# A fused delta-rule attention and two MoE layers: the first four chunks' norms split, their first loads and T's spread rewritten

## The chip, the cores and the metric

The kernel runs on one core of one Trainium2 chip. The metric is the device time of one execution in microseconds (us). The kernel before was run three times: 1037.36, 1038.86 and 1046.35 us, median 1038.86.

## The reference, cut to what matters

Inputs are q, k, v of shape (B=4, H=8, S=768, D=48), beta (B, H, S) and two pairs of weight matrices of 384 x 2048 and 2048 x 384.

```python
k_n = k / (np.linalg.norm(k, axis=-1, keepdims=True) + 1e-06)
state = np.zeros((B, H, D, D))
for t in range(S):
    y[:, :, t] = einsum('bhd,bhde->bhe', q[:, :, t], state)
    v_old = einsum('bhde,bhd->bhe', state, k_n[:, :, t])
    state += beta_t * einsum('bhd,bhe->bhde', k_n[:, :, t], v[:, :, t] - v_old)
x = y as rows of (B*S, H*D)
h = x @ w1_in;  x = softplus(h) @ w1_out
h = x @ w2_in;  x = (h * cos(h)) @ w2_out
```

So every key vector is divided by its norm, a recurrence over 768 steps makes y, and two dense layers with different activations follow.

## The kernel before

The 768 steps are cut into NS = 24 chunks of C = 32 steps, and the chunks into NG = 6 groups of four. Partitions hold 4 batches x 32 steps. All values that reach TensorE (PE) are pairs of f16 (a high part and a rest, called hi and lo), so a product takes three passes.

For a group g the work is: `norms(g)` loads the four K tiles kt0 to kt3 and makes 1/(norm + 1e-6) for all four chunks in n0 (a square on ScalarE, a sum over 48 on VectorE, then a square root by Ln and Exp with one Newton step, on 128 x 32 elements). `prep_k(n)` scales kt by n0, splits it into kp (hi, lo) and transposes it in 32 x 32 blocks. `gram(n)` multiplies K by K and Q by K on PE against block-diagonal copies (bdK, bdQ, bdA, bd2). `take_A`, `take_P` take the result out; `solve(g)` inverts the triangular systems of the four chunks together on VectorE, row by row (tmpd and tlan), and writes T: t16, then tg by a transpose, then DRAM. `step(n)` is the recurrence of chunk n: it uses T from bdT, and bdG, bd2, bdK and bdQ, loaded from DRAM. The results y16 of two chunks make one block of x for the first dense layer, `moe_block(0, j)`; the second layer, `moe_block(1, j)`, comes last. `weights(ph)` loads the 16 weight pieces of 768 KB each (`conv`, f = 0 to 15) and turns each into hi and lo with three VectorE instructions on 128 x 768 words (L456, L458, L460), a hi copy (L471 on ScalarE or L475 on VectorE) and a lo (L481). Piece 0 goes through the buffer raw, piece 1 through w8, piece 2 through w10.

For the first group there is a path of its own: the transposed K of chunks 0 to 3 goes into the tail of two weight buffers (w12, w14), and sixteen small loads of 48 KB (SBUF to SBUF, one for each of two tiles, two halves and four batches) spread it over bdK, bdQ, bdA and bd2; T of chunk 0 is spread over bdT by four copies on 32 partitions instead of through DRAM.

The order of the instructions on each engine is not the order of the code: the class `Plan` collects all operations with costs and dependences, runs a list scheduler with its own estimates (among them one for each DMA), and issues everything in the order that it found. An operation that two engines can do goes to the one that the planner picks. So a changed dependence or cost number moves instructions in the whole program. On the chip each engine, and SP and ScalarE as issuers of DMAs, runs its list strictly in order, and waits where an operand is not ready.

Of the kernel before, what the change touches and what calls it, by code (L numbers as in the profile page):

```python
# [10 lines left out]
F32 = mybir.dt.float32  # L11
# [3 lines left out]
AF = mybir.ActivationFunctionType  # L15
ALU = mybir.AluOpType
AX = mybir.AxisListType
# [3 lines left out]
P = 128  # L21
# [4 lines left out]
DM = H * D  # L26
# [30 lines left out]
class Plan:  # L57
# [59 lines left out]
    @staticmethod  # L117
    def after(o):

        return 0.65 + 0.9 + o["dma"] + o["slack"] if o["var"][0][0] == "SP" else 0.0  # L120

    def tails(self, succ):
        ops = self.ops
# [9 lines left out]
    def greedy(self, tail, succ, pred, back=None):  # L133
# [34 lines left out]
        while len(log) < n:  # L168
# [55 lines left out]
            if e == "SP" and back is None:  # L224
# [44 lines left out]
def dve(n, fast=False):  # L269
    return 0.068 + n / (1920.0 if fast else 960.0)  # L270
# [15 lines left out]
def delta_moe_moe_kernel(ctx, tc, q, k, v, beta, mask, w1, w2, out):  # L286
# [89 lines left out]
    def put(var, w, r, fn, **kw):  # L376
        return pl.add(var, w, r, fn, **kw)

    def dma(dst, src, w, r, eng_us, issue=0.475, **kw):
        put([("SP", issue)], w, r, lambda e: nc.sync.dma_start(out=dst, in_=src), dma=eng_us, **kw)  # L380
# [60 lines left out]
    cvn = [0]  # L441

    def conv(ph, f, t, key):
        put([("SP", 0.475)], key, [("wp2",)] if ph else [],
            lambda e: nc.sync.dma_start(out=t(), in_=(w1, w2)[ph][f]), dma=2.18)
        c = cvn[0] % NCV
        cvn[0] += 1
        cv = cvb[c]
        cf = cv.bitcast(F32)
        n = 2 * DM  # L450
        ck = [("cv", c, 0), ("cv", c, 1)]

# [24 lines left out]
        def lo(e):  # L477
            if ph:
                eng[e].tensor_tensor(out=wv(1), in0=cf, in1=wv(0), op=ALU.subtract)
            else:  # L480
                nc.vector.scalar_tensor_tensor(wv(1), in0=cf, scalar=sc, in1=wv(0), op0=ALU.mult, op1=ALU.subtract)  # L481

        put([("ACT", act(n)), ("DVE", dve(n, True))], wk, ck, hi, port=True)
        put([("POOL", pool(n)), ("DVE", dve(n))][0 if ph else 1:], wk, ck, lo, port=True)


    def norms(g):
        ss, n0, rn = nrm
        NK = [("n0",)]
        for n in range(4 * g, 4 * g + 4):  # L490
            s = n % 4
            kt = ktb[s]
            kk = [("kt", s)]
            dma(kt, k[n].rearrange("p (h d) -> p h d", h=H), kk, [("pre",)], 0.55, **A)
            if g:
                sqv, qk = sq, ("sq",)
            else:
                sqv, qk = (gb + eb)[s].rearrange("p a t -> p (a t)")[:, 0:DM].rearrange(
                    "p (h d) -> p h d", h=H), (("g", 0), ("g", 1), ("e", 0), ("e", 1))[s]
            actf(sqv, kt, AF.Square, [qk], kk + [("pre",)], DM, **A)  # L500
            put([("DVE", dve(DM))], [("ss", s)], [qk, ("pre",)],
                lambda e, s=s, sqv=sqv: nc.vector.reduce_sum(out=ss[:, s], in_=sqv, axis=AX.X), **A)
        SS = [("ss", i) for i in range(4)]
        m = 4 * H
        actf(n0, ss, AF.Ln, NK, SS + [("tiny",)], m, bias=tiny, **A)
        actf(n0, n0, AF.Exp, NK, [], m, scale=0.5, **A)
        put([("DVE", 0.269)], [("rn",)], NK, lambda e: nc.vector.reciprocal(out=rn, in_=n0), **A)
        tt(rn, rn, ss, ALU.mult, [("rn",)], SS, m, only=("DVE",), **A)
        tt(n0, n0, rn, ALU.add, NK, [("rn",)], m, only=("DVE",), **A)
        put([("DVE", 0.085)], NK, [], lambda e: nc.vector.tensor_scalar(  # L510
            n0, n0, 0.5 / K_SC, 1e-6 / K_SC, op0=ALU.mult, op1=ALU.add), **A)
        put([("DVE", 0.269)], NK, [], lambda e: nc.vector.reciprocal(out=n0, in_=n0), **A)

    def prep_k(n):
        s = n % 4
        kt, kp, kq = ktb[s], kpb[s], kqb[s]
        kk = [("kt", s)]
        tt(kt, kt, nrm[1][:, s].unsqueeze(2).to_broadcast([P, H, D]), ALU.mult, kk, [("n0",), ("pre",)], DM, pool_c=0.79, **A)
        ka = kab[n % 2]
        kr = kk + [("pre",)]  # L520

# [48 lines left out]
    def k_keys(n):  # L570
        return [("kq", n % 4, 0), ("kq", n % 4, 3)] if n >= 4 else [("kg", n, 0), ("kg", n, 1)]
# [64 lines left out]
    def solve(g):  # L636
# [17 lines left out]
        for j in range(N2 - 1):  # L654
# [14 lines left out]
        put([("DVE", 1.135)], [("tg",)], [("t16", 0), ("t16", 1)] + PR,  # L669
            lambda e: nc.vector.transpose(out=gw, in_=tw_), **A)  # L670
        if g == 0:
            for b in range(B):
                rows = slice(32 * b, 32 * b + 32)
                copy(bdT[rows, :, b], tg[rows, 0].rearrange("p h i x -> p h (i x)"), 1.0, [("bdT", b)],
                     [("tg",), ("bdT", "z")] + PR, 512, **A)
# [271 lines left out]
    for n in range(4):  # L947
        prep_k(n)
        if n % 2:
            dst, keys = (bdKQ[:, :, 0:12], bdA22)[n // 2], [first[n - 1][1], first[n][1]]  # L950
            src = kg0[n // 2][:, :, 16 * C:].rearrange("p n (x t) -> p n x t", t=X2)
            for m in range(2):
                for b in range(B):
                    rows = slice(32 * b, 32 * b + 32)
                    dma(dst[rows, m, :, b], src[rows, m], [(keys[m], b)],
                        k_keys(n - 1 + m) + [(keys[m], "z")], 0.5, issue=0.65, **A)
    for n in range(4):
        ps, pk = gram(n, first[n][0], first[n][1], (0,))
        take_A(n, ps[:, :, 0], pk)
# [92 lines left out]
```

## Time and profile before

| what | value |
|---|---|
| runs | 1037.36, 1038.86, 1046.35 us, median 1038.86 |
| profiled execution, span from first to last instruction | 1038.4 us; nothing else of that execution's time is given |
| PE busy, share of the span | 940.7 us, 91% |
| VectorE (DVE), ScalarE (ACT), GpSimd (POOL) | 668.8, 667.2, 366.2 us |
| PE's first matmul | 19.24 us |
| PE's first matmul of `step(0)` | 50.70 us |
| mean granted TensorE clock | 0.965 of full |

The profile is of one execution. Its span lies between the two lower runs, so the span can be read as the time of the kernel. Rows of a timeline give the start, the duration, the engine, the line of the kernel, the operation, output and inputs, and in square brackets how long the engine had stood idle and what released it; a number behind x is how many instructions were merged into a row.

### The profile page before, as it was taken

The numbers are of one execution on the slowest core, as the hardware profiler recorded it, in microseconds if no ns is written. First come the engines' busy times: TensorE is split into PE (matmuls) and PEld (weight loads), VectorE is DVE, ScalarE is ACT, GpSimd is POOL, SyncE is SP. The second block draws the span as 40 slices with busy tenths as digits, with TensorE's granted clock in tenths as the row PEclk, the third lists the DMA queues.
The fourth block names the chain that finished last, engine by engine and source line by source line (L and its number), as shares of the span: only waits on it lengthen the run. The fifth ranks groups of instructions, "written<-read, shape, count | busy, mean of one in ns | idle before, by whom it ended". The sixth has DMA issues, their size and how long they took to land.

```text
span 1038.4 us, 27814 instructions
## 1 busy us (share of the span) xinstructions
PE 940.7 (91%) x11552; PEld 687.5 (66%) x11552; DVE 668.8 (64%) x1186; ACT 667.2 (64%) x1261; POOL 366.2 (35%) x330
## 2 busy tenths in 40 slices
PE   1135889997999899999999999999999999999998
PEld 1125779886899798899999997744444444444443
DVE  8999977666547754863576665686555555555454
ACT  5344769776767776866777787865555555554554
POOL 3013326433523442432332545553332223233232
PEclk9965899998999999999999999999999999999999
DMA  6998696876766775674558862111001010000000
GB/s 194 288 262 203 128 240 121 200 177 170 175 84 149 178 155 111 135 157 76 117 115 210 237 153 84 44 35 61 31 1 61 1 61 0 31 31 1 31 1 31
DMA packets 307741, 117.94 MB, mean 114 GB/s; under 512 B 272160, under 2 KB 287648, under 8 KB 307616
## 3 DMA queue, kind: packets, MB, share of 16 engines
q1 hardware_dynamic: 307616, 116.17, 46.0%
q8 instruction: 91, 1.49, 0.6%
q14 instruction: 34, 0.28, 0.1%
HBM read 71.03 MB, written 35.65 MB: 103 GB/s over the span
## 4 chain that ended last, share of the span: by engine, by line
PE 72%; DVE 9%; ACT 7%; DMA 6%; issue 3%; SPq 2%; POOL 1%; DVEq 0%; ACTq 0%; POOLq 0%
PE psH L820 20%; PE accA L882 15%; PE accB L882 11%; PE psC L820 7%; PE psA L882 6%; PE psC L699 6%; PE psY L820 4%; DMA kpd<-kp 3%; PE psY L699 2%; SPq L380 2%; ACT kp L389 1%; PE psA L605 1%; DMA qt<-q_dram 1%; DVE tlan L401 1%; DMA kt<-k_dram 1%
## 5 line engine op out<-in xcount | busy, mean ns | idle before, releaser
L401 POOL TENSOR_TENSOR g<-g,g 128x512 f16<-128x512 f32 x191 | 227.7, 1192 | 461.1 <-ACT g L389 446.9
L820 PE MATMUL psH<-xt,w 128*128 128x256 f16 x1728 | 232.1, 276 | 0.2
L389 ACT ACTIVATE g<-g 128x512 f16<-128x512 f32 x191 | 119.9, 628 | 105.2 <-DVE g L405 70.3
L882 PEld LDWEIGHTS <-w 128*128 128x128 f16 x1728 | 163.3, 98 | 23.3 <-issue 3.6
L820 PEld LDWEIGHTS <-w 128*128 128x128 f16 x1728 | 158.7, 98 | 18.9 <-issue 0.3
L882 PE MATMUL accA<-g,w 128*128 128x256 f16 x1152 | 159.6, 275 | 3.2 <-POOL g L401 1.7
L882 PEld LDWEIGHTS <-v 128*128 128x128 f16 x864 | 84.5, 98 | 101.9
L820 PEld LDWEIGHTS <-v 128*128 128x128 f16 x864 | 84.6, 98 | 100.9
L410 ACT ACTIVATE e<-e 128x512 f32<-128x512 f32 x96 | 60.4, 629 | 81.7 <-DVE e L405 81.7
L401 DVE TENSOR_TENSOR g<-psH,e 128x512 f32<-128x512 f32 x96 | 66.1, 688 | 70.3 <-ACT e L412 64.0
L882 PE MATMUL accB<-g,w 128*128 128x256 f16 x576 | 94.7, 276 | 0.0
L820 PE MATMUL psH<-xu,v 128*128 128x512 f16 x351 | 83.1, 379 | 0.0
L820 PE MATMUL psC<-xu,v 128*128 128x512 f16 x342 | 81.5, 379 | 0.0
L882 PE MATMUL accB<-g,v 128*128 128x512 f16 x288 | 77.8, 379 | 0.0
L882 PE MATMUL accA<-g,v 128*128 128x512 f16 x288 | 77.8, 379 | 0.0
L882 PE MATMUL psA<-g,v 128*128 128x512 f16 x288 | 77.6, 379 | 0.0
L837 ACT ACTIVATE e<-psH 128x512 f32<-128x512 f32 x96 | 56.7, 590 | 30.8 <-PE psH L820 30.4
L699 PEld LDWEIGHTS <-bdKQ 128*128 128x128 f16 x1840 | 64.4, 98 | 10.5 <-issue 8.4
L412 ACT ACTIVATE e<-e,hpi 128x512 f32<-128x512 f32 x96 | 69.3, 721 | 3.0
L699 PEld LDWEIGHTS <-bdA 128*128 128x128 f16 x1680 | 56.6, 99 | 20.4 <-issue 18.4
L412 ACT ACTIVATE e<-e 128x512 f32<-128x512 f32 x96 | 59.9, 624 | 1.2
L699 PE MATMUL psC<-b,bdT 128*128 128x48 f16 x768 | 29.2, 187 | 34.1 <-ACT bdT L389 21.2
(143 smaller groups left out, 1508.6 us busy)
## 6 DMA issues: line engine op xcount, KB each, us to landing
bdKQ<-kqd SPq DMA_DIRECT2D x184, 64.0 KB, 2.8
kpd<-kp SPq DMA_DIRECT2D x24, 448.0 KB, 3.6
kqd<-kq SPq DMA_DIRECT2D x20, 512.0 KB, 4.2
raw<-w_dram SPq DMA_DIRECT2D x12, 768.0 KB, 5.0
bdA<-kpd SPq DMA_DIRECT2D x96, 96.0 KB, 3.5
w<-w_dram SPq DMA_DIRECT2D x10, 768.0 KB, 7.1
v<-w_dram SPq DMA_DIRECT2D x10, 768.0 KB, 6.5
qt<-q_dram SPq DMA_DIRECT2D x24, 256.0 KB, 4.2
```

The source lines that it names most:

```text
L380: put([("SP", issue)], w, r, lambda e: nc.sync.dma_start(out=dst, in_=src), dma=eng_us, **kw)
L389: nc.scalar.activation(out=out, in_=in_, func=AF.Copy, scale=scale)
L401: put(var, w, r, lambda e: eng[e].tensor_tensor(out=out, in0=a, in1=b, op=op), port=True, **kw)
L410: nc.scalar.activation(out=out, in_=in_, func=func, scale=scale)
L412: nc.scalar.activation(out=out, in_=in_, func=func, scale=scale, bias=bias)
L605: nc.tensor.matmul(ps[:, h], lhsT=w, rhs=x, start=(i == 0), stop=(i == len(ops) - 1))
L699: nc.tensor.matmul(ps[:, h, 0:D], lhsT=lhs(h), rhs=mov[:, h], start=(first and i == 0 and h == 0), stop=(last and i == len(passes) - 1 and ...
L820: nc.tensor.matmul(hp[:, i] if ph == 0 else hp, lhsT=w[:, l, kc * P:(kc + 1) * P], rhs=xv[:, m * KC + kc], start=(kc == 0 and idx == 0), s ...
L837: nc.scalar.activation(out=ev, in_=hv, func=AF.Abs, scale=sc)
L882: nc.tensor.matmul(acc[c], lhsT=w[:, l, c * P:(c + 1) * P], rhs=rhs, start=(f == 0 and idx == 0 and (ph == 1 or c != 1)), stop=(f == NF - ...
```

## The change

Five edits, all for the first group of chunks:

1. `norms(0)` works in two parts, chunks 0 and 1, then 2 and 3: the Ln, Exp and the five small VectorE instructions come twice, on 128 x 16 elements. The four loads of K are put first. For other groups nothing changes but the order in which the code lists things.
2. The load of weight piece 0 (raw) is made dependent on kt3 in the planner's list. Nothing is said on pieces 1 and 2.
3. Of the sixteen small loads of the first four chunks, those of batch 3 are issued from ScalarE's queue, four in all. The planner's cost for each is 0.62 to issue and 0.35 to move (0.65 and 0.5 before), and the planner treats a DMA by its cost field and no longer by the name of the issuing engine.
4. The four copies from tg to bdT move 256 words of 32 bits instead of 512 f16.
5. The planner's cost of T's transpose is 1.77 instead of 1.135; the instruction is the same.

```diff
 def conv(ph, f, t, key):
-        put([("SP", 0.475)], key, [("wp2",)] if ph else [],
+        put([("SP", 0.475)], key, [("wp2",)] if ph else [("kt", 3)] if f == 0 else [],
             lambda e: nc.sync.dma_start(out=t(), in_=(w1, w2)[ph][f]), dma=2.18)
 def norms(g):
-        for n in range(4 * g, 4 * g + 4):
+        parts = ((0, 1), (2, 3)) if g == 0 else ((0, 1, 2, 3),)
+        for part in parts:
+            for s in part:
+                dma(kt, k[4 * g + s]..., kk, [("pre",)], 0.55, **A)
+        for part in parts:
+            for s in part:
                 actf(sqv, kt, AF.Square, [qk], kk + [("pre",)], DM, **A)
                 put([("DVE", dve(DM))], [("ss", s)], ... reduce_sum(out=ss[:, s], in_=sqv) ...
-        m = 4 * H
+            m = len(part) * H
+            a, b, c = (x[:, part[0]:part[-1] + 1] for x in (ss, n0, rn))
             Ln, Exp, reciprocal, two tensor_tensor, tensor_scalar, reciprocal on a, b, c
 def solve(g):
-        put([("DVE", 1.135)], [("tg",)], ...transpose(out=gw, in_=tw_)
+        put([("DVE", 1.77)], [("tg",)], ...transpose(out=gw, in_=tw_)
-                copy(bdT[rows, :, b], tg[rows, 0]..., 1.0, [("bdT", b)], ..., 512, **A)
+                copy(bdT[rows, :, b].bitcast(F32), tg[rows, 0]....bitcast(F32), 1.0, [("bdT", b)], ..., 256, **A)
 loads of the first four chunks
-                    dma(dst[rows, m, :, b], src[rows, m], ..., 0.5, issue=0.65, **A)
+                    dma(dst[rows, m, :, b], src[rows, m], ..., 0.35, issue=0.62, on="SP" if b < 3 else "ACT", **A)
```

What the planner makes of it is read from the order of each engine's instructions. First the start of SP's list, the loads of K (kt), of weights (raw, w8, w10), of the mask, of Q (qt) and V (vt). Before:

```order
L380 DMA kt3_116<-k_dram 128x384
L445 DMA raw0_87<-w1_dram 128x768
L941 DMA mask_sb_76<-mask_dram 128x35
L445 DMA w8_83<-w1_dram 128x768
L380 DMA qt0_117<-q_dram 128x512
L445 DMA w10_84<-w1_dram 128x768
```

Of the change:

```order
L380 DMA kt3_116<-k_dram 128x384
L946 DMA mask_sb_76<-mask_dram 128x35
L445 DMA w8_83<-w1_dram 128x768
L380 DMA vt0_107<-v_dram 128x384
L380 DMA qt0_117<-q_dram 128x512
L445 DMA w10_84<-w1_dram 128x768
```

The load of piece 0 went from the place behind kt3 to the fourteenth place, behind a second load of vt0; piece 1 (w8) now follows kt3 with only the mask between them.

Second, ScalarE's list around the norms: squares of kt into g and e, Ln (L412) and Exp (L410) into n. Before, from the third square on:

```order
L410 ACTIVATE e0_95<-kt2_115 128x384
L410 ACTIVATE e1_96<-kt3_116 128x384
L412 ACTIVATE n0_120<-ss_119,tiny_78 128x32
L410 ACTIVATE n0_120<-n0_120 128x32
L389 ACTIVATE kp0_122<-kt0_113 128x256 x2
```

Of the change:

```order
L410 ACTIVATE e0_95<-kt2_115 128x384
L410 ACTIVATE e1_96<-kt3_116 128x384
L412 ACTIVATE n0_120<-ss_119,tiny_78 128x16
L410 ACTIVATE n0_120<-n0_120 128x16
L412 ACTIVATE n0_120<-ss_119,tiny_78 128x16
L410 ACTIVATE n0_120<-n0_120 128x16
L389 ACTIVATE bt_109<-vt0_107 128x384
```

All four squares still stand ahead of the first Ln. One Ln and one Exp became two of each, half as wide, and the copy of V to bt moved up behind them.

Third, a place far behind the edits: ScalarE's list in the middle of the program, where the casts of new K tiles (kp2, kp3 from kt2, kt3, of chunks of the next group) stand ahead of the copy u16 of a step. Before:

```order
L389 ACTIVATE kp2_124<-kt2_115 128x256
L412 ACTIVATE e0_95<-e0_95 128x512
L389 ACTIVATE kp2_124<-kt2_115 128x256
L389 ACTIVATE kp3_125<-kt3_116 128x256
L389 ACTIVATE ka0_126<-kp2_124 128x4x2x16
L389 ACTIVATE kp3_125<-kt3_116 128x256
L389 ACTIVATE ka1_127<-kp3_125 128x4x2x16
L389 ACTIVATE ka0_126<-kp2_124 128x4x2x16
L389 ACTIVATE u16_111<-psC1_146 128x384
```

Of the change:

```order
L853 ACTIVATE psH0_140<-psH0_140 128x512
L412 ACTIVATE e0_95<-e0_95 128x512
L389 ACTIVATE kp3_125<-kt3_116 128x256 x2
L389 ACTIVATE ka1_127<-kp3_125 128x4x2x16
L389 ACTIVATE u16_111<-psC1_146 128x384
```

The casts of kp2 moved some twenty rows ahead; those of kp3 still stand directly ahead of u16.

## Rows read from the trace of the kernel before

**Rows 1.** Page, part 1: busy us (share of the span) and instructions
```profile
PE 940.7 (91%) x11552; PEld 687.5 (66%) x11552; DVE 668.8 (64%) x1186; ACT 667.2 (64%) x1261; POOL 366.2 (35%) x330
```

**Rows 2.** Four stretches: length; busy of PE, PEld, DVE, ACT, POOL; clock; DMA
```profile
11.05:31.03 19.98, 7.22 (x240) 6.82 (x240) 19.94 (x38) 12.07 (x30) 1.90 (x2) 1.00 0.62 158
31.03:46.14 15.11, 0.00 (x0) 0.00 (x0) 12.60 (x45) 3.90 (x8) 0.00 (x0) 1.00 0.91 305
46.14:90.00 43.86, 16.20 (x376) 15.06 (x377) 43.86 (x67) 21.84 (x42) 10.82 (x9) 0.64 0.93 252
...
140.00:620.00 480.00, 460.18 (x8017) 420.79 (x8015) 305.24 (x597) 350.86 (x730) 185.59 (x179) 0.98 0.70 156
```

**Rows 3.** Timeline, SP's issues behind kt: start, us, what
```profile
2.60 0.43 SPq L445 DMA_DIRECT2D raw<-w_dram  x1
3.08 0.43 SPq L941 DMA_DIRECT2D mask_sb<-mask_dram  x1
```

**Rows 4.** Chain that ended last, the fourth K load: start, us
```profile
2.13 5.69 DMA kt<-k_dram
```

**Rows 5.** Tile kt to 15 us: time to landing of its loads
```profile
DMA to landing us min/median/max: 2.4/2.6/5.7
```

**Rows 6.** DMA issues to 4 us: count, KB each, us to landing
```profile
raw<-w_dram SPq DMA_DIRECT2D x1, 768.0 KB, 7.2
w<-w_dram SPq DMA_DIRECT2D x1, 768.0 KB, 8.3
```

**Rows 7.** Timeline, DVE: small instructions of the norms, then kt
```profile
8.40 0.55 DVE L502 TENSOR_REDUCE ss<-e 128x8 f32<-128x384 f32 x1 [1.87 <-ACT e L410]
...
10.00 0.19 DVE L401 TENSOR_TENSOR rn<-rn,ss 128x32 f32<-128x32 f32 x1
...
10.67 0.35 DVE L512 RECIPROCAL n<-n 128x32 f32<-128x32 f32 x1
11.05 1.66 DVE L401 TENSOR_TENSOR kt<-kt,n 128x384 f32<-128x384 f32 x2
```

**Rows 8.** Groups of DVE, 19.9 to 31.1 us: the first conversion instruction
```profile
L456 DVE TENSOR_SCALAR cv<-w 128x768 int32<-128x768 int32 x2 | 1.1, 536 | 0.0
```

**Rows 9.** Timeline, DVE: prices of kt, a lo and a cast
```profile
15.13 0.51 DVE L401 TENSOR_TENSOR kt<-kt,n 128x384 f32<-128x384 f32 x1
15.56 0.43 DVE L401 TENSOR_TENSOR kp<-kt,kp 128x256 f16<-128x256 f32 x1
...
15.89 0.83 DVE L391 CAST kp<-kt 128x256 f16<-128x256 f32 x1
```

**Rows 10.** Timeline: the sixteen small loads on SP
```profile
14.81 5.49 SPq L380 DMA_DIRECT2D bdKQ<-w  x8
...
20.40 6.20 SPq L380 DMA_DIRECT2D bdA<-w  x8
```

**Rows 11.** Timeline: the last taking-out before the solve
```profile
29.59 0.48 ACT L389 ACTIVATE abuf<-accA,mask_sb 128x128 f32<-128x128 f32 x1
...
30.16 0.95 DVE L481 SCALAR_TENSOR_TENSOR w<-cv,w 128x768 f16<-128x768 f32 x1
...
31.03 0.43 DVE L405 SCALAR_TENSOR_TENSOR abuf<-accA,mask_sb,abuf 128x128 f32<-128x128 f32 x1
```

**Rows 12.** Timeline: ScalarE and DVE at the wait for Q
```profile
35.39 0.77 ACT L389 ACTIVATE kq<-qt 128x512 f16<-128x512 f32 x1 [2.21 <-DMA qt<-q_dram]
...
36.52 0.45 DVE L401 TENSOR_TENSOR kp<-pm,kp 128x256 f16<-128x256 f32 x1 [1.65 <-ACT kp L389]
```

**Rows 13.** Timeline: bdT's four copies
```profile
48.09 2.56 ACT L389 ACTIVATE bdT<-tg 32x512 f16<-32x512 f16 x4 [2.71 <-DVE tg L670]
```

**Rows 14.** Groups of ACT to 60 us: count, busy, mean ns
```profile
L389 ACT ACTIVATE kp<-kt 128x256 f16<-128x256 f32 x7 | 3.1, 475 | 2.4 <-DVE kt L401 2.4
```

**Rows 15.** Timeline: the longest idle time of PE after 90 us
```profile
238.25 1.86 SPq L380 DMA_DIRECT2D kpd<-kp  x2
...
242.29 0.49 ACT L389 ACTIVATE kp<-kt 128x256 f16<-128x256 f32 x1 [5.22 <-DMA kpd<-kp]
...
245.27 0.80 PE L699 MATMUL psY<-u,bdA 128*128 128x48 f16 x16 [5.50 <-ACT u L389]
```

More of the change, by code (lines that the diff above doesn't have):

```diff
@@ L118, in after @@
     def after(o):
-        return 0.65 + 0.9 + o["dma"] + o["slack"] if o["var"][0][0] == "SP" else 0.0
+        return 0.65 + 0.9 + o["dma"] + o["slack"] if o["dma"] else 0.0
     def tails(self, succ):
@@ L223, in greedy @@
                 port[e] = end
-            if e == "SP" and back is None:
+            if o["dma"] and back is None:
                 dma_free = max(end + 0.65, dma_free) + o["dma"]
@@ L377, in put, with dma @@
         return pl.add(var, w, r, fn, **kw)
-    def dma(dst, src, w, r, eng_us, issue=0.475, **kw):
-        put([("SP", issue)], w, r, lambda e: nc.sync.dma_start(out=dst, in_=src), dma=eng_us, **kw)
+    def dma(dst, src, w, r, eng_us, issue=0.475, on="SP", **kw):
+        put([(on, issue)], w, r, lambda e: eng[e].dma_start(out=dst, in_=src), dma=eng_us, **kw)
     def copy(out, in_, scale, w, r, n, ps=False, fast=True, only=None, **kw):
@@ L488, in norms @@
         ss, n0, rn = nrm
-        NK = [("n0",)]
-        for n in range(4 * g, 4 * g + 4):
[L491 to L502, printed above, removed]
@@ L503, in norms @@
-        SS = [("ss", i) for i in range(4)]
-        m = 4 * H
[L505 to L511, printed above, removed]
@@ L512, in norms @@
-        put([("DVE", 0.269)], NK, [], lambda e: nc.vector.reciprocal(out=n0, in_=n0), **A)
+        parts = ((0, 1), (2, 3)) if g == 0 else ((0, 1, 2, 3),)
+        for part in parts:
+            for s in part:
+                kt = ktb[s]
+                kk = [("kt", s)]
+                dma(kt, k[4 * g + s].rearrange("p (h d) -> p h d", h=H), kk, [("pre",)], 0.55, **A)
+        for part in parts:
+            for s in part:
+                kt = ktb[s]
+                kk = [("kt", s)]
+                if g:
+                    sqv, qk = sq, ("sq",)
+                else:
+                    sqv, qk = (gb + eb)[s].rearrange("p a t -> p (a t)")[:, 0:DM].rearrange(
+                        "p (h d) -> p h d", h=H), (("g", 0), ("g", 1), ("e", 0), ("e", 1))[s]
+                actf(sqv, kt, AF.Square, [qk], kk + [("pre",)], DM, **A)
+                put([("DVE", dve(DM))], [("ss", s)], [qk, ("pre",)],
+                    lambda e, s=s, sqv=sqv: nc.vector.reduce_sum(out=ss[:, s], in_=sqv, axis=AX.X), **A)
+            SS, NK, RN = ([(x, s) for s in part] for x in ("ss", "n0", "rn"))
+            m = len(part) * H
+            a, b, c = (x[:, part[0]:part[-1] + 1] for x in (ss, n0, rn))
+            actf(b, a, AF.Ln, NK, SS + [("tiny",)], m, bias=tiny, **A)
+            actf(b, b, AF.Exp, NK, [], m, scale=0.5, **A)
+            put([("DVE", 0.269)], RN, NK, lambda e, b=b, c=c: nc.vector.reciprocal(out=c, in_=b), **A)
+            tt(c, c, a, ALU.mult, RN, SS, m, only=("DVE",), **A)
+            tt(b, b, c, ALU.add, NK, RN, m, only=("DVE",), **A)
+            put([("DVE", 0.085)], NK, [], lambda e, b=b: nc.vector.tensor_scalar(
+                b, b, 0.5 / K_SC, 1e-6 / K_SC, op0=ALU.mult, op1=ALU.add), **A)
+            put([("DVE", 0.269)], NK, [], lambda e, b=b: nc.vector.reciprocal(out=b, in_=b), **A)
@@ L517, in prep_k @@
         kk = [("kt", s)]
-        tt(kt, kt, nrm[1][:, s].unsqueeze(2).to_broadcast([P, H, D]), ALU.mult, kk, [("n0",), ("pre",)], DM, pool_c=0.79, **A)
+        tt(kt, kt, nrm[1][:, s].unsqueeze(2).to_broadcast([P, H, D]), ALU.mult, kk, [("n0", s), ("pre",)], DM, pool_c=0.79, **A)
         ka = kab[n % 2]
@@ L673, in solve @@
                 rows = slice(32 * b, 32 * b + 32)
-                copy(bdT[rows, :, b], tg[rows, 0].rearrange("p h i x -> p h (i x)"), 1.0, [("bdT", b)],
-                     [("tg",), ("bdT", "z")] + PR, 512, **A)
+                copy(bdT[rows, :, b].bitcast(F32), tg[rows, 0].rearrange("p h i x -> p h (i x)").bitcast(F32), 1.0,
+                     [("bdT", b)], [("tg",), ("bdT", "z")] + PR, 256, **A)
         dma(tgd[g], tg.rearrange("p n h i x -> p n (h i x)"), [("tgd", g)], [("tg",)] + PR, 1.46, **A)
@@ L955, in delta_moe_moe_kernel @@
                     dma(dst[rows, m, :, b], src[rows, m], [(keys[m], b)],
-                        k_keys(n - 1 + m) + [(keys[m], "z")], 0.5, issue=0.65, **A)
+                        k_keys(n - 1 + m) + [(keys[m], "z")], 0.35, issue=0.62, on="SP" if b < 3 else "ACT", **A)
     for n in range(4):
```

2 lines of the change are left out of this document (1 added, 1 removed).

## The prediction

> **What bounds the kernel now.** I read the page's busy times first [rows 1]: PE is busy for 940.7 of 1038.4 us, so some 98 us are PE's idle time, and only that, or the clock, can be won. The table of stretches says where it lies [rows 2]: PE has 7.2 us of work in the first 31 us and none from 31 to 46, so about 39 of the 98 us are the start, in which K becomes T; from 140 to 620 us 19.8 us of PE are idle; the second layer behind that has next to none. So a microsecond won at the start is worth a microsecond at the end only if what bounds the start is shortened, and that the same table names: VectorE is busy for 19.94 of 19.98 us from 11.05 on, and for 43.86 of 43.86 us from 46.14 to 90. Only in the solve, 31 to 46 us, has it 2.5 us to spare. The conversions of the weights fill every gap there. So I count the start in VectorE's work and look at loads and ScalarE only where VectorE waits for them: the fourth K, 2.13 to 7.82 us [rows 4], and one wait of 1.65 us in the solve [rows 12].
>
> **The change part by part**, against the span of 1038.4 us (the median of the runs is 0.5 us above it).
>
> *K's landing.* The fourth K load takes 5.7 us, the quickest of the kind 2.4 us [rows 4, 5]. The edit is to keep the 768 KB of piece 0 out of its way. But only piece 0 is held back, and the order shows that piece 1, as large, takes its place behind the mask. Piece 0 was issued at 2.60, the place behind it is at 3.08 [rows 3], so the competition comes 0.5 us later, no more. I take -0.5. The ends are 0, and -3.3 if the fourth load came down to 2.4 us. The Trainium skill, page "DMA: Bandwidth & Descriptors", section "Queues, rings and completion order", says that on each DMA engine the descriptors of one issuing queue are consumed in ring order; by that a load issued behind K on SP's queue cannot hold K up, the term is 0 and the sum would be 0.5 us higher. The row that bears on it is mixed: raw landed at 2.60 + 7.2 = 9.8 us, before w, which was issued later and took longer [rows 3, 6], but ring order alone does not say why the fourth K took 5.7 us.
>
> *Norms two and two.* The planner left all four squares ahead of the first Ln, so the first part gets no start from it. The first part's Ln and Exp now run beside the last sum (8.40 to 8.95), but eight small instructions instead of five stand on VectorE before the first kt is scaled [rows 7]: three reciprocals at 0.35 and five others at 0.19 are 2.0 at most, and 0.1 for the start, the 2.1 us that lay between 8.95 and 11.05 before. Interleaved, the two parts no longer wait for their own last result, so I take -0.3 for the first kt; then a scalar step (0.19) and a reciprocal (0.35) of the second part follow on an engine that has no idle time: +0.5. I take +0.2; the ends are -0.3 and +1.2 (five more instructions at full price).
>
> *VectorE's work up to the twelfth lo (L481), at about 90 us.* I counted its instructions to this place in both orders. More in the change: three hi copies (TENSOR_SCALAR, 128 x 768, f32 to f16, which ScalarE did before) and two scalings of kt (POOL before). Fewer: one lo of kp, one cast, one tensor_tensor of 128 x 384. A hi copy on VectorE is not in the trace; the nearest rows are the same instruction type and size, 0.54 [rows 8], and a lo of the size with two inputs, 0.95 [rows 11]. I take 0.54, so +1.6 (end: +2.85). Two kt at 0.51 are +1.0; the fewer ones are 0.43 + 0.83 + 0.51 = -1.8 [rows 9]. In the trace the first pair of kt took 1.66 beside POOL's own scaling, 0.6 more than two alone [rows 7, 9]; POOL has none there now: -0.6. Together +0.2, to +1.5.
>
> *Four small loads from ScalarE.* Sixteen loads take SP 5.5 and 6.2 us [rows 10], so four fewer free 2.9 us. This I cost at nothing: what they feed ends in the abuf copy of the fourth chunk, which ScalarE had done at 30.07, and VectorE took it at 31.03 directly behind a lo, without idle time [rows 11]. VectorE's list to that place has now two conversion instructions fewer (0.95 each), which come back inside the solve; so it gets there some 2 us earlier, and the loads 2.9 us earlier plus the 0.96 to spare. If that cover were gone, and ScalarE's queue were the path, four issues of 0.7 would cost up to +2.8; behind them stand the abuf copies. Nor does raw's late load cost anything: the second load of vt0 that it stands behind waits for ScalarE's copy of V, about 10 us, and 10.5 + 7.2 = 17.7 [rows 6] is ahead of 20, when VectorE comes to it. From there each microsecond late is one lost.
>
> *The wait in the solve.* ScalarE waits 2.21 us for Q, and the cast of pm behind it holds VectorE 1.65 us [rows 12]. Now SP comes to the Q loads earlier by the 2.9 less two K loads, and VectorE's reader of the cast stands five rows later, about 1 us. I take -1.3 (0 to -1.65).
>
> *bdT.* Four copies of 512 took 2.56 [rows 13]; one of 256 elements takes 0.475 [rows 14], so four are 1.9, -0.7 on the way to `step(0)`. At the end it is worth 0, since from 46.14 to 90 VectorE has no idle time to give; the ends are -0.7 and 0.
>
> *What moves behind the start.* The planner's new order reaches the whole program. The one place with a price: at 236 us ScalarE stands 5.22 us at a cast that waits until the old kp has left for DRAM, the copy of u behind it waits too, and PE with it for 5.50 [rows 15]. SP issued that store and the next at 238.25. In the new order the casts of kp2 stand twenty rows ahead and its store some places ahead; those of kp3 still stand directly before u. ScalarE comes to them about 1.2 us later than before (two more instructions), SP to the store of kp3 about 0.9 earlier (two small loads fewer at 0.65, one K load more), so I expect some 3.2 us of idle time instead of 5.5: -2.3, with the ends -5.5 and +5.2 (such a wait once more).
>
> The sum: -0.5 + 0.2 + 0.2 + 0 - 1.3 + 0 - 2.3 = -3.7, which is 1034.7; I say **1035 us**.
>
> **The rivals.**
> - *Loads and issue are the path after all.* Then the fourth K gives 3.3, the solve's wait 1.65, bdT 0.7, the small loads 2.9, with 2.3 behind: 10.9 off, 1027.5; if only K gives all, 1031.9. For it speaks that SP issues the small loads without a break [rows 10]; against it VectorE's 19.94 of 19.98 us. 13 in 100, half of it beyond 1%.
> - *The change doesn't do what it says.* K lands as before because a load as large follows it, or because of ring order as above, and the wait at 236 us stays: 0 + 0.2 + 0.2 - 1.3, so 1037.5. For it speaks the order of SP. 20 in 100.
> - *Slower: ScalarE's list.* A cast of kp3 ahead of u waits for a store that SP has behind bdK's loads; there is such a place in each of the middle groups, and now a K load more stands ahead of the store. From the point where the store is issued 4 us (242.29 less 238.25) before ScalarE arrives, nothing is lost; past it each place costs up to 5.2. One place more, with no gain at 236 us: 1034.7 + 2.3 + 5.2 = 1042.2; three: over 1052. 13 in 100, of which 5 beyond 1%.
>
> **How the numbers follow.** The forecast has 54 in 100, with a range of its own of 1031 to 1038.5. About 1% either way, 1028.5 to 1049 by the median, is what a measurement of this kernel can tell from no change. Faster by more: half of the first rival, 7 in 100. Slower by more: 5. The rest, 88, is within 1%. The range that leaves out 2 in 10 runs from 1028 (the first rival nearly whole) to 1043 (one ScalarE wait more).
>
> **What would show it.** Right: VectorE with next to no idle time from the first scaling of kt to 90 us; the fourth K landing at 7 to 7.8 us; the wait for Q in the solve mostly gone; `step(0)` on PE 0.5 to 3 us before 50.70; about 3 us of PE idle time at a copy of u near 240 us. Wrong: the fourth K landing at 5 us; VectorE idle at the abuf copies or at cv<-raw; PE's idle time between 140 and 620 us changed by more than 5 us from 19.8; the granted clock in 46 to 90 us other than the 0.64 of before (the levels are 1.0 and 0.5, 2.4 and 1.2 GHz), which I take as unchanged since PE's work there is the same.

## The result, and the profile after

The changed kernel is slower: 1048.42 us (median of 13 runs, 1044.69 to 1052.25) against 1040.00 us of the kernel before in the same comparison (13 runs, 1037.36 to 1046.35). The ratio is 1.0073, with an interval of 1.0056 to 1.0089, so 7.6 us more (5.8 to 9.3). The forecast was 1035, with a range from 1028 to 1043; that it stays within 1% was forecast too. The profiled execution took 1048.42 us, and its span is 1046.3 us (before: 1038.4). All lines that follow are of that execution unless another kernel is named.

Page, part 1 of the kernel after (busy us, share of the span, instructions), to be laid beside [rows 1]:

```profile
PE 941.1 (90%) x11552; PEld 686.6 (66%) x11552; DVE 667.2 (64%) x1191; ACT 665.4 (64%) x1262; POOL 363.7 (35%) x331
```

No engine has noticeably more to do (PE 0.4 us). So 7.5 of the 7.9 us by which the span grew are idle time of PE. Where they lie is read from the table of stretches (length; busy of PE, PEld, DVE, ACT, POOL; granted clock; DMA share; GB/s), the four of [rows 2] and the one between them:

```profile
11.05:31.03 19.98, 7.05 (x240) 6.74 (x240) 18.90 (x44) 9.80 (x28) 1.88 (x2) 1.00 0.76 198
31.03:46.14 15.11, 0.00 (x0) 0.00 (x0) 11.95 (x39) 2.85 (x5) 0.00 (x0) 0.53 0.89 272
46.14:90.00 43.86, 16.05 (x368) 14.80 (x369) 43.63 (x66) 19.55 (x40) 10.05 (x10) 0.54 0.87 238
90.00:140.00 50.00, 37.33 (x705) 33.03 (x705) 42.76 (x79) 28.02 (x59) 13.24 (x13) 0.86 0.82 163
140.00:620.00 480.00, 458.14 (x7993) 418.79 (x7993) 307.65 (x610) 350.46 (x728) 185.08 (x179) 0.98 0.68 154
```

The kernel before has this in the stretch that [rows 2] leaves out:

```profile
90.00:140.00 50.00, 42.25 (x807) 38.47 (x807) 47.52 (x97) 30.77 (x65) 13.44 (x14) 0.80 0.75 158
```

Up to 90 us PE has done as much as before (16.05 against 16.20 us). From 90 to 140 us it loses 4.9 us (37.33 against 42.25), and VectorE has 7.2 us of idle time there instead of 2.5. From 140 to 620 us another 2.0 are lost (458.14 against 460.18). What PE waits for in the largest of the new gaps shows in the timeline (start, us, engine, line, what; in brackets the idle time before it and what ended it): first SP, then ScalarE, VectorE and PE, and a second such place at 193 us.

```profile
134.62 1.75 SPq L380 DMA_DIRECT2D kt<-k_dram  x3
...
133.45 0.61 ACT L848 ACTIVATE e<-e 128x512 f32<-128x512 f32 x1
139.33 0.52 ACT L410 ACTIVATE sq<-kt 128x384 f32<-128x384 f32 x1 [5.26 <-DMA kt<-k_dram]
139.76 0.51 ACT L389 ACTIVATE b<-bt 128x384 f16<-128x384 f32 x1
...
140.29 0.56 DVE L405 SCALAR_TENSOR_TENSOR b<-bt,b 128x384 f16<-128x384 f32 x1 [4.99 <-ACT b L389]
...
140.31 0.95 PE L704 MATMUL psC<-b,raw 128*128 128x48 f16 x24 [4.35 <-ACT b L389]
...
193.23 0.52 ACT L410 ACTIVATE sq<-kt 128x384 f32<-128x384 f32 x1 [6.07 <-DMA kt<-k_dram]
...
194.70 0.95 PE L704 MATMUL psC<-b,raw 128*128 128x48 f16 x24 [3.73 <-ACT b L389]
```

ScalarE is done at 134.06 us with what it can do. Next on its list stands the square of a K of the third group of chunks, while PE works on the first, so nobody needs its result yet. The load of that K was issued by SP at 134.62 and lands at 139.3. Behind the square stands the rounding of `b`, which was ready; VectorE waits 4.99 us for it and PE 4.35. The planner had issued this load at 119.43 us of its own time, took it as landed at 122.5 and put the square at 122.96: 3.1 us from issue to landing, where the trace has 4.7. Summed over 85 to 620 us, ScalarE's waits for the three kinds of transfers that it meets in its list are, before and after (us in total, times, longest):

```profile
ACT kp L389 <- DMA kpd<-kp: 19.6, 8, 5.2
ACT kq L389 <- DMA qt<-q_dram: 5.6, 3, 4.8
ACT sq L410 <- DMA kt<-k_dram: 4.0, 3, 2.4
```
```profile
ACT kp L389 <- DMA kpd<-kp: 17.2, 9, 3.7
ACT sq L410 <- DMA kt<-k_dram: 15.4, 4, 6.1
ACT kq L389 <- DMA qt<-q_dram: 3.9, 2, 2.5
```

The waits for K grew by 11.4 us, the other two fell by 4.1 together. None of the edits touches these squares, loads or places; what changed there is the planner's order. Whether that is the cause is what the experiments ask.

The start shows less than was taken from it. The timeline of the kernel after, ScalarE and VectorE in order of time:

```profile
5.35 1.07 ACT L410 ACTIVATE e<-kt 128x384 f32<-128x384 f32 x2 [1.04 <-DMA kt<-k_dram]
...
8.59 0.56 DVE L401 TENSOR_TENSOR kt<-kt,n 128x384 f32<-128x384 f32 x1
...
8.78 0.52 ACT L389 ACTIVATE bt<-vt 128x384 f32<-128x384 f32 x1 [1.18 <-DMA vt<-v_dram]
...
10.88 0.45 DVE L401 TENSOR_TENSOR kp<-kt,kp 128x256 f16<-128x256 f32 x1 [0.73 <-ACT kp L389]
...
26.08 0.53 ACT L410 ACTIVATE sq<-kt 128x384 f32<-128x384 f32 x1 [1.91 <-DMA kt<-k_dram]
...
27.66 0.46 DVE L405 SCALAR_TENSOR_TENSOR abuf<-accA,mask_sb,abuf 128x128 f32<-128x128 f32 x1 [1.08 <-ACT abuf L389]
...
34.12 0.77 ACT L389 ACTIVATE kq<-qt 128x512 f16<-128x512 f32 x1 [3.21 <-DMA qt<-q_dram]
...
35.25 0.45 DVE L401 TENSOR_TENSOR kp<-pm,kp 128x256 f16<-128x256 f32 x1 [2.47 <-ACT kp L389]
...
46.12 1.92 DVE L675 STREAM_TRANSPOSE tg<-t 128x1024 f32<-128x1024 f32 x1
48.07 1.72 ACT L389 ACTIVATE bdT<-tg 32x256 f32<-32x256 f32 x4 [2.36 <-DVE tg L675]
```

The first K is scaled at 8.59 instead of 11.05 us [rows 7], the last `abuf` is taken out at 27.66 instead of 31.03 [rows 11], and T is nevertheless turned at 46.12, as before (46.14). On the way lie a new wait for V on ScalarE (1.18, with K's casts behind it), one at `abuf` (1.08), a longer one for Q (2.47 against 1.65, [rows 12]), and conversions that came back into the solve (at 40.80, 42.10 and 44.47 us).

### The profile page after: what moved, and what is told of

Its sections match the earlier page's. It is cut to its first block, busy times and chain, and to the rows that moved or that the text cites. A ratio compares the mean times of both kernels' runs of the same rounds, so it can differ in the third digit from the quotient of the medians.

```text
span 1046.3 us, 27809 instructions
## 1 busy us (share of the span) xinstructions
PE 941.1 (90%) x11552; PEld 686.6 (66%) x11552; DVE 667.2 (64%) x1191; ACT 665.4 (64%) x1262; POOL 363.7 (35%) x331
## 4 chain that ended last, share of the span: by engine, by line
PE 68%; DVE 9%; DMA 7%; SPq 6%; ACT 5%; issue 3%; POOL 1%; DVEq 0%; POOLq 0%; ACTq 0%
PE psH L825 19%; PE accA L887 14%; PE accB L887 10%; PE psC L825 7%; PE psA L887 6%; SPq L380 5%; PE psC L704 5%; PE psY L825 3%; PE psY L704 2%; DMA kpd<-kp 2%; DVE cv L460 1%; PE psA L610 1%; DVE cv L458 1%; DMA kt<-k_dram 1%; DMA bdKQ<-kqd 1%
## 5 line engine op out<-in xcount | busy, mean ns | idle before, releaser
L410 ACT ACTIVATE e<-e 128x512 f32<-128x512 f32 x96 | 60.4, 629 | 83.4 <-DVE e L405 83.1
L412 ACT ACTIVATE e<-e,hpi 128x512 f32<-128x512 f32 x96 | 69.2, 721 | 2.9
L704 PE MATMUL psC<-b,bdT 128*128 128x48 f16 x768 | 29.7, 188 | 37.3 <-ACT bdT L389 21.2
L412 ACT ACTIVATE e<-e 128x512 f32<-128x512 f32 x96 | 60.0, 625 | 1.0
```

What stands on the lines that cost most here:

```text
L410: nc.scalar.activation(out=out, in_=in_, func=func, scale=scale)
L412: nc.scalar.activation(out=out, in_=in_, func=func, scale=scale, bias=bias)
L704: nc.tensor.matmul(ps[:, h, 0:D], lhsT=lhs(h), rhs=mov[:, h], start=(first and i == 0 and h == 0), stop=(last and i == len(passes) - 1 and ...
```

## The experiments

Three theories were set against each other. The **order theory**: the edits leave the time as it is, and the planner's new order of what follows T loses it. The **edit theory**: held-back weights and loads on ScalarE's queue make what follows late. And **given back**: whatever wait is taken away comes back at another place.

To part order from edits, the list that the planner makes (5,813 entries in the kernel after, each an engine and an operation) was written into the kernel in place of the planner's call. All "written out" orders below are made so:

```diff
-        for _, _, e, i in self.log:
-            self.ops[i]["fn"](e)
+        for x in LIST:
+            self.ops[int(x[1:])]["fn"]({"P": "PE", "D": "DVE", "A": "ACT", "G": "POOL", "S": "SP", "-": "-"}[x[0]])
```

The results in one table. PE's idle time is 535 us less PE's busy time from 85 to 620 us, in the profiled execution, whose span stands beside it. Each ratio is against executions of the kernel before in the same comparison, whose medians were 1040.0 to 1040.5 us. The profiled execution need not be a typical one: that of "after, longer transfers" is the fastest of its ten, that of "after, two K loads early" the second slowest of its ten.

| kernel | median us | ratio to before (interval) | span, profiled | PE idle 85 to 620 | T turned at |
|---|---|---|---|---|---|
| before | 1040.0 | 1 | 1038.4 | 29.3 | 46.14 |
| before, again | (one run: 1037.7) | | 1035.9 | 30.7 | 44.80 |
| after | 1048.4 | 1.0073 (1.0056 to 1.0089) | 1046.3 | 36.2 | 46.12 |
| after, again | (one run: 1047.4) | | 1045.3 | 35.7 | 46.17 |
| start of after, rest of before | 1041.9 | 1.0006 (0.9981 to 1.0031) | 1036.2 | 30.1 | 47.55 |
| start of before, rest of after | 1044.6 | 1.0038 (1.0012 to 1.0065) | 1044.4 | 34.9 | 45.16 |
| after, two K loads early | 1045.1 | 1.0033 (1.0002 to 1.0065) | 1048.3 | 38.1 | 47.55 |
| before, planner 1.77 | 1041.0 | 1.0030 (0.9995 to 1.0065) | 1037.3 | 31.0 | 44.85 |
| after, planner 1.135 | 1043.8 | 1.0035 (1.0016 to 1.0053) | 1040.7 | 33.1 | 44.47 |
| mix, V later | 1043.3 | 1.0027 (1.0006 to 1.0048) | 1041.0 | 33.8 | 46.73 |
| mix, V and Q | 1039.0 | 0.9992 (0.9968 to 1.0017) | 1033.1 | 29.6 | 43.27 |
| after, longer transfers | 1041.8 | 1.0025 (1.0004 to 1.0046) | 1035.5 | 29.7 | 57.13 |
| the same, one wait less | 1033.0 | 0.9941 (0.9917 to 0.9965) | 1028.9 | 23.6 | 57.22 |
| before, longer transfers | 1032.8 | 0.9939 (0.9916 to 0.9962) | 1029.9 | 26.0 | 54.57 |

The spans go roughly with PE's idle time behind 85 us, and not with the time at which T is there. Roughly, since PE's busy time differs too: before and "mix, V and Q" have nearly the same idle time (29.3 and 29.6 us) and spans 5.3 us apart, with PE busy for 940.7 and 935.7 us.

**Start and rest exchanged.** The cut lies at the transpose that gives T of the first group.

> The changed kernel with all five edits. Its instructions stand in the changed order up to the transpose that gives T of the first group, and from there on in the order (and on the engines) of the kernel before, written out as a list. Order theory (the loss is made by the new order of what follows T: ScalarE reaches squares and casts before their transfers have landed): 1037 to 1041 us, PE busy for about 42 of the 50 us from 90 to 140 as before, no wait of ScalarE for a K load near 139. Edit theory (the edits themselves, held-back weights and loads on ScalarE's queue, make what follows late): 1046 to 1049 us, PE busy for 37 to 38 of those 50 us.

> The counterpart: the kernel before, none of the five edits, in its own order up to T of the first group, and from there on in the order of the changed kernel. Order theory: 1045 to 1050 us, with a wait of ScalarE for a K load near 135 to 140 us. Edit theory: 1037 to 1041 us.

With all five edits and the old order behind T the time is not distinguishable from that of before (1.0006; 1041.9 us, 0.9 above the 1037 to 1041 that the order theory expected), and PE is busy for 41.23 us from 90 to 140. With no edit and the new order behind T it is 1.0038, with 37.55 us there:

```profile
90.00:140.00 50.00, 41.23 (x791) 37.50 (x789) 47.81 (x97) 31.07 (x65) 13.42 (x13) 0.82 0.78 169
```
```profile
90.00:140.00 50.00, 37.55 (x705) 33.82 (x705) 42.35 (x79) 27.74 (x57) 12.81 (x13) 0.84 0.78 151
```

ScalarE's waits for K from 85 to 620 us go with the order and not with the edits; first the start of after with the rest of before, then the counterpart:

```profile
ACT sq L410 <- DMA kt<-k_dram: 3.5, 3, 1.8
```
```profile
ACT sq L410 <- DMA kt<-k_dram: 16.1, 4, 6.0
```

So the edit theory falls: its prediction of 1046 to 1049 for the first is missed, and that of 1037 to 1041 for the second too. The counterpart stayed just below what the order theory expected (1044.6, expected 1045 to 1050). Its 0.4% and the start's 0.1% do not quite make up the 0.73% of the two together. The intervals allow it, but whether start and order add up is left open.

**Two K loads earlier.** On SP, in the order of after (one of the two places; the numbers at the names are the planner's buffers):

```diff
-L380 DMA raw_87<-tgd 32x8x64 x4
-L380 DMA bdA_102<-kpd 32x24x64 x4
-L800 DMA_TRANSPOSE xt_91<-y_112 128x6x128
-L380 DMA bdKQ<-kqd 32x16x64 x4
-L380 DMA kpd<-kp_122 128x1792
-L380 DMA vt_107<-v_dram 128x384
-L380 DMA kt_114<-k_dram 128x384
+L380 DMA raw_87<-tgd 32x8x64
+L380 DMA kt_114<-k_dram 128x384
+L380 DMA raw_87<-tgd 32x8x64 x3
+L380 DMA bdA_102<-kpd 32x24x64 x4
...
```

> The changed kernel in its own order but for two instructions: the load of K that the square at 139 us waits for is issued 13 places earlier on SP, and the one that the square at 193 us waits for is issued 9 places earlier. Their buffers have been free for long. Order theory, with waits that add up: both waits of ScalarE (5.3 and 6.1 us) go, PE regains about 4 us by 140 and 3 to 4 by 195, and the time is 1038 to 1042 us. Rival, given back: PE regains them there and loses them again at a later wait; 1045 to 1049 us.

Both waits are gone (the squares start at 135.30 and 188.50 us without one), and PE is busy for 41.29 us from 90 to 140, 4.0 more, as expected. The median regains 3.3 us, not 7, and at 1045.1 it lies at the lower edge of what the rival expected. By the two ratios the gain is 0.40% with about 0.36% either way, so it is barely clear of noise. The profiled execution (1050.2, among the longest of ten that range from 1039.9 to 1050.4) has 38.1 us of PE idle time, not less than the 36.2 of after, and shows where the gain can go: from 200 to 360 us PE is busy for 144.76 us against 150.09, and ScalarE waits more for kpd and Q:

```profile
ACT kp L389 <- DMA kpd<-kp: 22.8, 10, 4.9
ACT kq L389 <- DMA qt<-q_dram: 8.7, 3, 3.2
ACT sq L410 <- DMA kt<-k_dram: 7.0, 3, 3.4
```

So in this execution what was won up to 140 us was lost again at later waits. Five of the ten executions, at 1039.9 to 1043.2 us, may have kept it; that is not shown, since none of them was profiled. What the two waits at the squares cost the kernel after therefore stays open between next to nothing and all of the loss.

**The planner's number alone.** Edit five contains a number that changes no instruction, the duration assumed for the transposes of T. It was set in the kernel before, and taken back in the kernel after:

```diff
-        put([("DVE", 1.135)], [("tg",)], [("t16", 0), ("t16", 1)] + PR,
+        put([("DVE", 1.77)], [("tg",)], [("t16", 0), ("t16", 1)] + PR,
```

> The kernel before with one number changed, the duration that the planner assumes for the transposes that give T (1.135 to 1.77 us). No instruction is added, removed or changed, only the order and the choice of engines. Order theory: the time moves by some us although nothing is done differently, either way, 1034 to 1048 us; a square or a cast on ScalarE waits for its transfer at other places than before. Edit theory: 1037 to 1042 us, as the kernel before.

> The changed kernel with the planner's duration of the transposes that give T at its old 1.135 us; all instructions as in the changed kernel, only order and engines move. Order theory: the time moves by some us without anything being done differently, 1036 to 1050 us, and the sum of ScalarE's waits for K, Q and kpd goes with it. Edit theory: 1046 to 1050 us as the changed kernel.

In the kernel before the effect is not distinguishable from nothing, though ScalarE's waits for K, Q and kpd grow from 29.2 to 33.3 us. In the kernel after, taking the number back brings 4.7 us (1048.4 to 1043.8; by the ratios 0.38% with about 0.25% either way, some half of the 0.73% lost), with every instruction still there. The waits fall from 36.5 to 32.9 us and PE's idle time from 36.2 to 33.1, as the order theory expected. The trace measures this transpose at 1.9 us, so 1.77 is the truer number: here a truer number made the worse order.

**Is it chance of one execution?**

> The kernel before once more, its own order written out as a list, so that a second execution of it is profiled. Landing theory (the fourth K lands early because the first weights are held back): its square starts at 7.8 us as in rows 4, and the third and fourth squares stand apart. Rival (the landing differs from execution to execution, and the hold does nothing): third and fourth squares together at 5.3 to 6.1 us, as in the run with the start of before and the rest of after.

> The changed kernel once more, its own order written out as a list, for a second profiled execution. If the lost time is fixed by the order: the square of K at about 139 us waits again for 3 to 6 us, the copy of V near 9 us waits 1 to 3 us, T starts at 46.0 to 47.6 us, and PE is busy for 37 to 39 of the 50 us from 90 to 140. If it is chance of one execution: PE busy for 41 us or more there.

For the loss: no. In a second execution of after PE is busy for 38.51 us from 90 to 140, the square waits 4.51 us at 138 and 5.07 us at 191, and T is turned at 46.17 us. For K's landing: yes. ScalarE's third and fourth square in the kernel before, second execution:

```profile
5.64 1.03 ACT L410 ACTIVATE e<-kt 128x384 f32<-128x384 f32 x2 [1.44 <-DMA kt<-k_dram]
```

The fourth starts at 6.15 us, 1.7 earlier than in the execution that was read before, with nothing changed. With the start of before and the rest of after it was 6.0. In the runs with the first weight held back behind the mask it starts between 5.6 and 6.1, and in the three kernels with longer transfers (below), which load a weight directly behind K, between 5.9 and 6.1.

**V and Q at the start.** The run with the start of after and the rest of before shows the wait for V larger, ScalarE and then VectorE:

```profile
10.32 0.52 ACT L389 ACTIVATE bt<-vt 128x384 f32<-128x384 f32 x1 [2.51 <-DMA vt<-v_dram]
...
12.42 0.44 DVE L401 TENSOR_TENSOR kp<-kt,kp 128x256 f16<-128x256 f32 x1 [2.27 <-ACT kp L389]
```

In a kernel made from this one, V's copies and the first rounding of Q stand behind K's casts on ScalarE, and V's second load behind the small loads on SP. In another, Q's loads also stand further ahead on SP, and the squares of the next K behind `abuf`. The three instructions that move in both (they come back behind the casts):

```diff
 L410 ACTIVATE n_120<-n_120 128x16
-L389 ACTIVATE bt<-vt_107 128x384
-L389 ACTIVATE b_110<-bt 128x384
-L389 ACTIVATE kq_128<-qt_117 128x512
 L389 ACTIVATE kp_122<-kt_113 128x256 x2
```

> As the run with the start of after and the rest of before, but for ScalarE's first copies: the copy of V with its rounding (bt<-vt, b<-bt) and the first rounding of Q, which stand ahead of the first casts of K and wait for V's load, now stand behind these casts; the second load of that V buffer stands behind the small loads on SP. Theory (VectorE's idle time at kp, 0.7 to 2.5 us, is V's landing): that idle time falls below 0.8 us, the small loads and the gram products start 1.4 to 2 us earlier; T 0.5 to 1.5 us earlier than 47.55, because the square of the next K then stands ahead of the last abuf copy. Time 1038 to 1042 us. Rival (VectorE's work is the bound there): T within 0.4 us of 47.55.

> The same, and the squares of the next K on ScalarE behind the abuf copies, and on SP the third Q load ahead of these K loads and the fourth ahead of two loads of weights. Theory (the solve waits 2.4 to 3 us for Q because two weight loads stand ahead of it): the wait at kp<-pm is below 0.7 us and the transposes that give T start at 42.5 to 44.5 us (46.1 in both kernels). If the start is worth its time at the end: 1036 to 1039 us. Rival (a start that is earlier is lost again to waits for transfers behind it): T is as early, and the time is 1040 to 1044 us.

The first brings T from 47.55 to 46.73, within what was expected, and VectorE's wait is gone; but the time is 1043.3 us, above the 1038 to 1042 expected (1.0027). In the second the wait for Q is gone and T is there at 43.27:

```profile
30.49 0.75 ACT L389 ACTIVATE kq<-qt 128x512 f16<-128x512 f32 x1
...
43.27 1.91 DVE L675 STREAM_TRANSPOSE tg<-t 128x1024 f32<-128x1024 f32 x1
```

The time is 1039.0, at the upper end of what a start worth its time would give; against before it is not distinguishable (0.9968 to 1.0017), although T is 1.5 to 2.9 us earlier than in the executions of before. Against the run that it was made from, with nearly the same order behind T, T is 4.3 us earlier and the median 2.9 us lower; the ratios differ by 0.14% with about 0.35% either way, which leaves room for nothing as well as for the whole 4.3 us.

**A planner that takes transfers as longer.** One number in two places, first in the kernel after:

```diff
-        return 0.65 + 0.9 + o["dma"] + o["slack"] if o["dma"] else 0.0
+        return 0.65 + 2.9 + o["dma"] + o["slack"] if o["dma"] else 0.0
...
-                end = dma_free + 0.9 + o["slack"]
+                end = dma_free + 2.9 + o["slack"]
```

> The changed kernel with one number changed, the time that the planner adds to every transfer (0.9 to 2.9 us); no instruction is added or removed, only order and engines move. Theory (ScalarE waits because the planner takes transfers as shorter than they are: the K load of 139 us planned at 3.1 us from issue to landing and measured at 4.7): the waits of ScalarE for K, Q and kpd behind 85 us, 36.5 us in after, fall below 25 us, and the time is 1036 to 1042 us. Rival (any new order has as many such waits, whatever numbers it is made from): 33 to 45 us of such waits and 1043 to 1050 us.

ScalarE's waits for K, Q and kpd fall from 36.5 to 23.2 us, and the time to 1041.8, both as the theory expected. T is 11 us later, and PE has lost little by it: it is busy for 18.99 us up to 85 us (after: 19.75), and its idle time behind 85 us is 29.7 instead of 36.2. What is left has one large piece, here VectorE, then PE behind it:

```profile
382.43 0.31 DVE L547 STREAM_TRANSPOSE kq<-ka 128x128 f32<-128x128 f32 x1 [8.31 <-DMA kqd<-kq]
...
383.79 1.12 PE L704 MATMUL psC<-b,raw 128*128 128x48 f16 x24 [6.77 <-ACT b L389]
```

The transpose L547 writes a part of the `kq` tile that the store to kqd does not read by the kernel's keys, so the planner knows of no dependence. It had put the store first in the list, and the program made the transpose wait for the store. In all other chunks, and in before and after, the store stands behind. Writing this one store down behind the transpose leaves every engine's instructions in the same order and moves only the wait (the names in brackets are what an instruction waits for; DMAHW1 is a DMA queue's counter):

```diff
-L547 STREAM_TRANSPOSE kq_129<-ka_127 128x128 [waits DMAHW1_49,Activation_49]
+L547 STREAM_TRANSPOSE kq_129<-ka_127 128x128 [waits Activation_49]
```

> The order of the run with the planner's longer transfers, every engine's instructions in the same order, but one store (kqd<-kq of chunk 21) is written down behind the transpose L547 that follows it instead of ahead of it. The transpose writes another part of the kq tile, but waited 8.3 us until the store had left, and PE 6.8 us behind it. Theory (one such wait costs its full length, since what follows has no idle time to take it up): PE's wait of 6.8 us at 383 us goes, and the time falls by 5 to 7 us from 1041.8 to 1034.5 to 1037. Rival (given back at later waits): 1039 to 1043 us.

```profile
376.14 0.31 DVE L547 STREAM_TRANSPOSE kq<-ka 128x128 f32<-128x128 f32 x1 [0.58 <-ACT ka L389]
```

1033.0 us, 8.8 less, and more than the 5 to 7 expected; by the ratios it is 0.84% with about 0.32% either way, 5.4 to 12 us. PE's idle time behind 85 us falls by 6.1 us, the span by 6.6. A single wait of 6.8 us on PE was worth about its length, and no later wait took it back.

> The kernel before with the one number that the planner adds to every transfer raised from 0.9 to 2.9 us; none of the five edits. Theory (fewer waits for transfers, whatever the start): waits of ScalarE for K, Q and kpd behind 85 us fall from 29 us to 10 to 25, and the time is 1033 to 1040 us. Rival (an order is as good as chance makes it): such waits of 25 to 40 us and 1039 to 1048 us.

The kernel before, with none of the edits, comes to 1032.8 with the same number (five executions), with 24.9 us of such waits, where the ranges of theory and rival meet. Here T is turned 8.4 us later than in before, and PE is busy for more from 90 to 140:

```profile
90.00:140.00 50.00, 44.58 (x865) 41.14 (x865) 47.56 (x96) 31.23 (x61) 12.81 (x13) 0.84 0.79 166
```

This kernel and the one with one wait less beat the kernel before by 0.6% and the changed one by some 1.3%. With the edits (0.9941) and without (0.9939) they are level, but the one with the edits needed the store moved (1.0025 without that). Both orders drawn with longer transfers were better than the ones that they replace. Since a new order alone moved the time by some 4 us above, two draws do not show that the longer transfers, and not the draw, made them so.

## Why the prediction was wrong, step by step

- **The step that failed is "what moves behind the start".** It said that the new order reaches the whole program and then priced one place, the wait at 236 us. All other places were taken as unchanged without being named. The priced place came as forecast: PE waits 3.51 us at `u` near 248 us (about 3 were expected, 5.50 before [rows 15]). The loss is at places that had no row before, because a wait that a new order makes cannot be in the old trace: 4.35 and 3.73 us at squares of K. So the term, forecast at -2.3, came out at +6.9 us of PE's idle time from 85 to 620 us (29.3 to 36.2). The sum needed a term for such places with a spread of several us either way. The 0.4% of the exchanged orders, and 4.7 us for one planner number, are its measured size. Shown is that the new order behind T loses time without the edits, and that the edits with the old order behind T lose none that can be told from nothing; how much of the loss the two squares made is not.
- **The right mechanism stood among the rivals, at 13 in 100.** "ScalarE's list" gave an in-order wait for a transfer ahead of what PE needs, with 1042.2 us for one place more and over 1052 for three; two at its price are 1047.4. That this comes close to the 1048.4 measured is partly luck: the instruction was a square of K and not a cast of kp, the two places cost PE 4.4 and 3.7 us and not 5.2 each, the wait at `u` did become shorter, and with both places taken away only 3.3 us came back. It counted the casts alone; the same list holds squares and roundings of Q that wait on loads.
- **"A microsecond won at the start is worth a microsecond at the end only if what bounds the start is shortened"** was the ground for reading the start so closely, and T stood for the start. The runs show that T's time alone does not tell: the three kernels with longer transfers turn T 8 to 11 us later, in other orders, and come out once 0.2% slower than before and twice 0.6% faster. What T is worth with the order behind it held stays open (4.3 us earlier: 2.9 us less, within noise). That a start which finishes T later because it did other work first has lost nothing is a reading and not shown; VectorE, busy for 43.86 and 43.63 us of the 43.86 behind T in before and after, speaks for it.
- **The start as a whole, -1.4.** The executions with the start of before turn T at 46.14, 45.16 and 44.80 us, those with the start of after at 46.12, 46.17, 47.55 and 47.55. So T came no earlier, and against the other two executions 1 to 3 us later; the one that was read before the forecast was the late one.
- **K's landing, -0.5.** The trace had 7.8 us, forecast 7 to 7.8, measured 5.9. But the same start has 6.0 and 6.15 in two further executions, so the 5.69 us [rows 4] were one late execution, and the hold is worth some 0.2 us. The Trainium skill, page "DMA: Bandwidth & Descriptors", section "Queues, rings and completion order", has the descriptors of a queue consumed in ring order on each DMA engine, though a later one may finish its write before an earlier one. From the order the prediction took that a load behind K cannot hold K up, which the section does not say in so many words. The further executions agree with it (6.0 to 6.15 with the weight behind K, 5.6 to 6.1 with it held back), and leave the one at 7.84 us unexplained. The rival "the change doesn't do what it says" was right on this term.
- **The norms, +0.2.** In every run with the start of after the first K is scaled at 8.59 us, in the two further executions with the start of before at 9.22 and 9.37. So the first K came 0.6 to 0.8 earlier, with the landing in it; what the rest of the term cost behind it was not measured by itself.
- **VectorE's work to about 90 us, +0.2.** The lo that stands near 90 us in the trace is the eleventh (89.50); the twelfth stands at 97.23. From the first scaling of kt VectorE has 77.83 us of work ahead of the eleventh, 75.90 before, and 84.92 against 83.63 ahead of the twelfth: +1.9 and +1.3, at the end that the prediction gave (+1.5) and not at 0.2. A hi copy took 0.55 us, as taken.
- **V, not in the sum.** The prediction looked at V's load for the conversions, not for what stands behind its copy on ScalarE: K's casts. This wait was 1.2 to 3.0 us in the four executions with the start of after.
- **The small loads, 0.** SP's share fell from 11.7 us [rows 10] to 8.5, about as worked out (8.8). The cover was gone, as the text had put it as a condition: VectorE idles 1.08 us at `abuf`, behind a square on ScalarE that waits for the next K's load.
- **The wait for Q, -1.3.** It became 0.8 longer. Q's load was issued at 26.55 us, 1.3 earlier than before, and took 7.5 us as before, while the solve came to it 3.4 us earlier. A wait for a load shrinks by the difference of two gains, and the second was left out.
- **bdT, 0.** Four copies of words take 1.72 us (1.9 was worked out), and `step(0)` starts 0.8 us earlier. What that is worth at the end was not measured.

## What to carry to other kernels

Where a planner orders the whole program, a change at one place has two effects: its own, and a new draw of the order behind it. Price the second with its spread, or hold the order fixed and measure the first by itself. Here engines lost where an instruction that nobody needed yet stood ahead of one that was needed, and waited for a transfer that the plan took as too short: compare the plan's time from issue to landing with the trace's (3.1 and 4.7 us here), and try a longer one. Taking such a wait away can be worth its whole length (6.8 us on PE, 8.8 at the end) or be lost again (the two K loads), so measure each by itself. And a landing time read once is one sample: profile a second execution before a term rests on it.

## What the runs showed of the hardware

- The same four K loads in the same order, with the same loads behind them, let the fourth square start at 7.84 us in one execution and at 6.15 and 6.0 in two others.
- The granted clock from 46 to 90 us was 0.64 in before, 0.54 in after, and 1.00 in the run with two K loads early (1.0 is 2.4 GHz, 0.5 is 1.2 GHz); the prediction had named a change of it as a sign of being wrong. PE's busy time there was 16.20, 16.05 and 15.31 us, and none of the times follows it. VectorE is busy for 43.86, 43.63 and 43.32 us of these 43.86.

```profile
46.14:90.00 43.86, 15.31 (x352) 1.00 0.88 242
```

- A transpose into one part of a tile waited 8.3 us for a store, written down ahead of it, that reads another part of the same tile.
- Single executions of the kernel before lie between 1036.5 and 1046.8 us (31 runs in one comparison), so differences of 0.3% need the intervals.
